# Routed attention with a feed-forward block: the mask products on row tiles of 32 rows in place of 64

## The chip, the cores and the metric

The kernel runs on one core of a Trainium2 chip. The metric is the time of one execution on the device in microseconds. The kernel before was run three times: median 895.17 us, 894.86 to 895.47. One more execution was taken with the hardware profiler; the views below come from it.

## The reference

Queries, keys and values have 4 batches, 8 heads, 768 positions and 64 numbers per head, in float32. Each head has 16 centroids. Every query and every key is assigned to the centroid with the largest cosine, and a query sees only the keys of its own cluster:

```
q_assign = np.argmax(np.einsum('bhsd,hcd->bhsc', q_n, c_n), axis=-1)
k_assign = np.argmax(np.einsum('bhsd,hcd->bhsc', k_n, c_n), axis=-1)
mask = q_assign[:, :, :, None] == k_assign[:, :, None, :]
scores = scale * np.matmul(q, k.transpose(0, 1, 3, 2))
scores = np.where(mask, scores, -1000000000.0)
attn = softmax(scores)            # max taken off, exp, divided by the sum
out = np.matmul(attn, v)
```

The heads are then joined to rows of 512, and a layer norm, a product with 512x2048 weights, a ReLU, a product with 2048x512 weights and an addition of the input follow (the feed-forward part).

## The kernel before

**Heads go in pairs.** There are 16 pairs (4 batches, 4 pairs of heads). The queries of a pair lie transposed in one tile of 128 rows, `t0`, and the keys in another, `t1`: rows 0 to 63 hold the 64 numbers of the first head, rows 64 to 127 those of the second; the 768 positions are the columns. The queries are taken in two halves of 384 columns (`HC`), the keys in 6 blocks of 128. A *step* `(n, g, c)` is pair n, half g, key block c: 16 x 2 x 6 = 192 steps, and the six steps of one half make a *half pair* (a "unit" in the code), 32 in all.

**A step** (`scores`, lines 368 to 389) fills one PSUM tile `s_ps` with two banks, one for each head. It does so with four products on TensorE (line 386):

- two *mask products* in bf16, head j = 0 and j = 1. Their operands are the one-hot cluster tiles `mask[0]` (queries) and `mask[1]` (keys). Each head owns 64 rows of these tiles, from row j * 64 on. Of these, the first 32 (`Q`) hold its one-hots for 16 clusters and those of the other half or head, scaled by 0 or 1; the other 32 rows are set to zero. The key side holds 0 or -2^100, so a pair of positions in different clusters gets a number that the exponential turns into zero.
- two *q·k products* in f32, which are added onto the same banks.

Then ScalarE takes the exponential of both heads at once (line 381, tile `e`). The slice that both kinds of product use is

```
rows = [slice(j * D, (j + 1) * D) for j in range(2)]
```

with D = 64, so head 0 works on rows 0 to 63 and head 1 on rows 64 to 127 of TensorE's array. Such a product occupies a *tile* of the array, 64 rows by 128 columns; products on different rows can run side by side.

**Weighing** (`weigh`, line 398) multiplies the exponentials by v, over 128 rows, into columns 0 to 63 for head 0 and 64 to 127 for head 1 (tiles of 128x64). `finish` (line 452) sums the denominators with tiles of 128x32, and `prep_sims` (line 305) computes the similarities to the centroids, also with tiles of 128x32. `prep_mask` (lines 349 to 355) writes the mask tiles of the next pair. Line 671, `busy`, issues idle products of 128x128 at the start.

**The order is written out by hand** (`manual_schedule`). At the start, three steps are prepared (`AHEAD` = 3): three times q·k alone, then three times the masks with the exponential. Then, for each half pair, come the scores of its six steps (three in the first half pair), one behind the other, each with its mask products ahead of its q·k products; then, in the first half of a pair, the denominators of the pair before and the similarities of the next; then the six weighings. The first mask of a half pair therefore comes behind other products (nearly always weighing), every other mask behind the q·k products of the step before.

**The feed-forward part** follows the attention. Its products (lines 803, 910 and 1093) use the whole array, 128x128.

In the profile PE is TensorE's products, PEld its weight loads. An f32 product shows as two weight loads and two matmul records; a bf16 product shows as one of each.

Of the kernel before, what the change touches and what calls it, by code (L numbers as in the profile page):

```python
# [19 lines left out]
def kernel(  # L20
# [12 lines left out]
    B, H, S, D = q.shape  # L33
# [7 lines left out]
    Q = 32  # L41
# [101 lines left out]
    mask = [heads.tile([P, S], BF16, name=f"mask_{i}", bufs=1) for i in range(2)]  # L143
# [224 lines left out]
    def scores(i, first="mask", parts=("mask", "qk", "exp")):  # L368
        n, g, c = steps[i]
        st = prepared[n]  # L370
        if parts[0] == first:
            st["s", i] = ps_s.tile([P, 2, 512], F32, tag="s", name="s_ps")
        s = st["s", i]
        keys = slice(c * P, (c + 1) * P)
        rows = [slice(j * D, (j + 1) * D) for j in range(2)]
        for part in parts:
            if part == "exp":
                if c % 2 == 0:
                    soft[i // 2] = attn.tile([P, 2, 2, HC], F32, tag="e", name="e", bufs=4)
                e = soft[i // 2][:, c % 2]  # L380
                nc.scalar.activation(e, s[:, :, :HC], AF.Exp, scale=SCALE)  # L381
                continue
            for j in range(2):
                of_queries, of_keys = [(mask if part == "mask" else st)[i][rows[j]] for i in range(2)]
                o = (g ^ j if part == "mask" else g) * HC
                nc.tensor.matmul(  # L386
                    s[:, j, :HC], of_keys[:, keys], of_queries[:, o : o + HC],
                    start=part == first, stop=part != first, skip_group_check=True,
                )
# [119 lines left out]
    rows = {}  # L509
# [155 lines left out]
    with tc.manual_schedule(engines=order | {mybir.EngineType.SP}):  # L665
# [25 lines left out]
        for i in range(AHEAD):  # L691
            scores(i, "qk", ("qk",))
        for i in range(AHEAD):
            scores(i, "qk", ("mask", "exp"))
        load_weight(0)
        load_weight(1)
    with tc.manual_schedule(engines=order | {mybir.EngineType.Pool}):
        for u in range(len(pairs) * slots):
# [9 lines left out]
            for i in own:  # L708
                if i >= AHEAD:
                    scores(i)  # L710
# [609 lines left out]
    with tc.manual_schedule(engines={mybir.EngineType.PE}):  # L1320
        st = {}
# [319 lines left out]
```

## Time and profile before

| what | value |
|---|---|
| median of three runs | 895.17 us |
| the profiled execution, its own time | 896.45 us |
| span of the profiled execution, first to last instruction | 894.6 us |
| mean granted clock of TensorE | 0.998 |
| first and last product of line 386 start at | 9.0 and 324.7 us |
| q·k products (s_ps<-t,t) | 768 records, 154.9 us, mean 483 ns |
| mask products (s_ps<-mask,mask) | 384 records, 63.0 us, mean 324 ns |
| weighing (a_ps<-e,v_sb) | 768 records, 130.9 us, mean 490 ns |
| weight loads of q·k, of the mask | mean 188 ns, mean 94 ns |
| exponentials (line 381, ScalarE) | 192, 151.2 us, mean 813 ns |

A line of a group gives the source line, the engine and the operation, the tiles written and read, the shapes, the count, the busy time in us and the mean length of one record in ns. In the timeline a line is a start, the length of the merged group from its first start to its last end, and a count. Records of products that follow each other overlap, because the array takes in the next product while the last one drains; how fast products follow each other is seen from the differences of their starts. In a table by stretches each engine has its busy time and the count of instructions, in the order PE, PEld, VectorE, ScalarE, GpSimd, followed by the granted clock and the share and rate of the DMA.

### The profile page before, as it was taken

The numbers are of one execution on the slowest core, as the hardware profiler recorded it, in microseconds if no ns is written. First come the engines' busy times: TensorE is split into PE (matmuls) and PEld (weight loads), VectorE is DVE, ScalarE is ACT, GpSimd is POOL, SyncE is SP. The second block draws the span as 40 slices with busy tenths as digits, with TensorE's granted clock in tenths as the row PEclk, the third lists the DMA queues.
The fourth block names the chain that finished last, engine by engine and source line by source line (L and its number), as shares of the span: only waits on it lengthen the run. The fifth ranks groups of instructions, "written<-read, shape, count | busy, mean of one in ns | idle before, by whom it ended". The sixth has DMA issues, their size and how long they took to land.

```text
span 894.6 us, 13278 instructions
## 1 busy us (share of the span) xinstructions
PE 879.7 (98%) x4724; PEld 576.6 (64%) x4724; DVE 701.5 (78%) x1158; ACT 399.7 (45%) x739; POOL 79.3 (9%) x143
## 2 busy tenths in 40 slices
PE   8999999999999999999999999999999999999995
PEld 4444444444444445568886558997557997557995
DVE  6999989899888888889555777897646897645774
ACT  4777777898877753331003552102553111333110
POOL 1122222112111212110000000000000000000000
PEclk9999999999999999999999999999999999999999
DMA  7889999999797536877423558963236862511875
GB/s 154 151 184 176 161 167 193 220 197 180 159 217 129 146 90 181 202 189 244 163 73 134 195 196 302 306 178 91 48 86 183 286 204 54 98 72 36 270 200 99
DMA packets 250489, 147.86 MB, mean 165 GB/s; under 512 B 193568, under 2 KB 209072, under 8 KB 249392
## 3 DMA queue, kind: packets, MB, share of 16 engines
q1 hardware_dynamic: 234784, 130.75, 56.3%
q0 software_dynamic: 7776, 15.03, 8.6%
q10 hardware_dynamic: 7856, 1.16, 0.8%
q8 instruction: 39, 0.64, 0.3%
q14 instruction: 34, 0.28, 0.1%
HBM read 105.25 MB, written 33.25 MB: 155 GB/s over the span
## 4 chain that ended last, share of the span: by engine, by line
PE 64%; DVE 0%; issue 0%
PE x_ps L803 18%; PE x_ps L1093 12%; PE z_ps L803 9%; PE z_ps L1093 6%; PE x_ps L910 5%; PE y_ps L803 5%; PE y_ps L1093 3%; PE z_ps L910 2%; PE y_ps L910 1%; PE s_ps L386 1%; PE a_ps L398 1%; PE den_ps L452 0%; DVE u L1108 0%; DVE y_end L1194 0%; DVE m L1108 0%
## 5 line engine op out<-in xcount | busy, mean ns | idle before, releaser
L381 ACT ACTIVATE e<-s_ps 128x768 f32<-128x768 f32 x192 | 151.2, 813 | 8.8 <-PE s_ps L386 5.0
L386 PE MATMUL s_ps<-t,t 64*128 64x384 f32 x768 | 154.9, 483 | 0.0
L398 PE MATMUL a_ps<-e,v_sb 128*64 128x384 f32 x768 | 130.9, 490 | 0.0
L398 PEld LDWEIGHTS a_ps<-e,v_sb 128*64 128x64 f32 x768 | 52.3, 137 | 75.8 <-issue 62.8
L386 PEld LDWEIGHTS s_ps<-t,t 64*128 64x128 f32 x768 | 68.2, 188 | 34.6 <-issue 33.6
L1093 PE MATMUL x_ps<-lower,w 128*128 128x192 f32 x448 | 80.9, 327 | 1.2 <-DVE u L1108 0.9
L1093 PEld LDWEIGHTS x_ps<-lower,w 128*128 128x128 f32 x448 | 74.0, 190 | 3.1 <-DVE u L1108 1.5
L834 DVE TENSOR_TENSOR lower<-z_ps,u 128x384 f32<-128x384 f32 x56 | 31.0, 553 | 54.7 <-PE z_ps L803 45.9
L386 PE MATMUL s_ps<-mask,mask 64*128 64x384 bf16 x384 | 63.0, 324 | 1.1 <-ACT e L381 0.7
L842 ACT ACTIVATE lower<-lower 128x384 f32<-128x384 f32 x88 | 45.0, 522 | 40.3 <-DVE lower L834 40.3
L433 DVE TENSOR_TENSOR two<-e 128x1536 f32<-128x1536 f32 x30 | 52.6, 1753 | 13.0 <-ACT e L381 12.9
L829 ACT COPY u<-x_ps 128x384 f32<-128x384 f32 x64 | 30.6, 479 | 68.1 <-PE x_ps L803 68.1
L829 ACT COPY p<-x_ps 128x384 f32<-128x384 f32 x32 | 15.1, 471 | 91.1 <-PE x_ps L803 91.1
L436 DVE TENSOR_TENSOR two<-two,e 128x1536 f32<-128x1536 f32 x30 | 52.6, 1752 | 1.7
L386 PEld LDWEIGHTS <-mask 64*128 64x128 bf16 x384 | 19.4, 94 | 42.7 <-issue 11.7
L803 PE MATMUL x_ps<-xn,w 128*128 128x384 f32 x128 | 46.6, 487 | 0.0
L803 PE MATMUL x_ps<-xn,ws 128*128 128x384 f32 x128 | 46.5, 486 | 0.0
L803 PE MATMUL y_ps<-xn,w 128*128 128x384 f32 x128 | 46.5, 486 | 0.0
L803 PE MATMUL x_ps<-xt,ws 128*128 128x384 f32 x128 | 46.5, 486 | 0.0
L803 PE MATMUL z_ps<-xt,ws 128*128 128x384 f32 x128 | 46.5, 486 | 0.0
L803 PE MATMUL x_ps<-xt,w 128*128 128x384 f32 x128 | 46.5, 486 | 0.0
L803 PE MATMUL z_ps<-xn,ws 128*128 128x384 f32 x128 | 46.5, 486 | 0.0
(210 smaller groups left out, 1486.7 us busy)
## 6 DMA issues: line engine op xcount, KB each, us to landing
w<-w_d SPq DMA_DIRECT2D x84, 256.0 KB, 3.7
raw<-in_moe_w_ch_dram SPq DMA_DIRECT2D x32, 512.0 KB, 5.7
w<-w_t SPq DMA_DIRECT2D x36, 256.0 KB, 5.0
w<-tb POOLq DMA_DIRECT2D x32, 256.0 KB, 6.6
w_d<-wt SPq DMA_DIRECT2D x7, 1024.0 KB, 4.7
w<-w_all SPq DMA_DIRECT2D x27, 256.0 KB, 3.0
v_sb<-in_v_dram SPq DMA_DIRECT2D x32, 192.0 KB, 4.7
xr<-x_d SPq DMA_DIRECT2D x24, 256.0 KB, 3.1
```

What stands on the lines that cost most here:

```text
L381: nc.scalar.activation(e, s[:, :, :HC], AF.Exp, scale=SCALE)
L386: nc.tensor.matmul(s[:, j, :HC], of_keys[:, keys], of_queries[:, o : o + HC], start=part == first, stop=part != first, skip_group_check=True,)
L398: nc.tensor.matmul(acc[j * D : (j + 1) * D, :HC], loaded[n]["v"][:, j, c, :], e[:, j, :], start=(c == 0), stop=(c == NT - 1),)
L433: nc.vector.tensor_tensor(two, soft.pop(u), soft.pop(u + 1), ALU.add)
L436: nc.vector.tensor_tensor(two, two, soft.pop(u + 2), ALU.add)
L803: nc.tensor.matmul(bank[:, :HC], lhs[:, c, :], rhs[:, c], start=first and c == 0, stop=c == NDH - 1, skip_group_check=True,)
L829: nc.scalar.copy(t, bank[:, :HC])
L834: nc.vector.tensor_tensor(h, bank[:, :HC], other, ALU.add)
L842: nc.scalar.activation(h, h, AF.Relu)
L910: nc.tensor.matmul(bank[:, :MH].rearrange("p (h f) -> p h f", h=2), hidden[lhs + (c,)][:, tt * P : (tt + 1) * P], rhs[:, :, c], start=firs ...
L1093: nc.tensor.matmul(bank, w[:, c, :], a[:, c], start=way in (1, 2, 5) and c == 0, stop=c == NQH - 1, skip_group_check=True,)
```

## The change

One line of `scores` is replaced by two. The mask products take 32 rows for each head, the one-hots alone: rows 0 to 31 for head 0 and 64 to 95 for head 1. The q·k products keep their 64 rows.

```
             for j in range(2):
-                of_queries, of_keys = [(mask if part == "mask" else st)[i][rows[j]] for i in range(2)]
+                r = slice(j * D, j * D + Q) if part == "mask" else rows[j]
+                of_queries, of_keys = [(mask if part == "mask" else st)[i][r] for i in range(2)]
                 o = (g ^ j if part == "mask" else g) * HC
                 nc.tensor.matmul(
                     s[:, j, :HC], of_keys[:, keys], of_queries[:, o : o + HC],
```

The tile of the array that a product occupies follows from its operands' rows, so the mask products go from tiles of 64x128 (at rows 0 and 64) to tiles of 32x128 (at rows 0 and 64). Line numbers behind the change are one higher in the changed kernel.

More of the change, by code (lines that the diff above doesn't have):

```diff
@@ L383, in scores @@
             for j in range(2):
-                of_queries, of_keys = [(mask if part == "mask" else st)[i][rows[j]] for i in range(2)]
+                r = slice(j * D, j * D + Q) if part == "mask" else rows[j]
+                of_queries, of_keys = [(mask if part == "mask" else st)[i][r] for i in range(2)]
                 o = (g ^ j if part == "mask" else g) * HC
```

## The prediction

> **What bounds the kernel now.** I read the page's busy shares first, then the busy time by stretches, then TensorE's own waits, and last the instructions one by one where TensorE changes from one kind of product to another.
>
> The page, parts 1 and 2:
>
> ```profile
> span 894.6 us, 13278 instructions
> PE 879.7 (98%) x4724; PEld 576.6 (64%) x4724; DVE 701.5 (78%) x1158; ACT 399.7 (45%) x739; POOL 79.3 (9%) x143
> PE   8999999999999999999999999999999999999995
> ```
>
> A busy share alone doesn't prove a bound, since the ends of matmuls are modelled. So I took the attention by itself (18.6 to 310.6 us), and then the list of what PE waited for between 18 and 308 us, which has one line:
>
> ```profile
> 18.60:310.60 292.00, 290.67 (x2069) 133.52 (x2069) 269.54 (x354) 233.22 (x356) 59.56 (x92) 1.00 0.88 175
> PE s_ps L386 <- ACT e L381: 0.2, 1, 0.2
> ```
>
> PE is busy for 290.67 of 292.00 us, at a granted clock of 1.00, and waits for others for 0.2 us. VectorE with 269.54 and ScalarE with 233.22 have room. After the attention the feed-forward part keeps PE as full (554.26 of the 565 us behind 330). So each nanosecond that PE gains or loses in the attention arrives at the end undiminished; no engine stands by to hide it.
>
> The steady rhythm of the scores, from the timeline of PE (start, length of the merged group, count):
>
> ```profile
> 203.98 0.33 PE L386 MATMUL s_ps<-mask,mask 64*128 64x384 bf16 x2
> 204.14 0.81 PE L386 MATMUL s_ps<-t,t 64*128 64x384 f32 x4
> 204.79 0.33 PE L386 MATMUL s_ps<-mask,mask 64*128 64x384 bf16 x2
> ```
>
> Count by starts, not by lengths, because one matmul's record overlaps the next. A step takes 204.79 - 203.98 = 0.81 us: 0.16 for the two mask products, 0.65 for the two q·k products. Each f32 product is two weight loads and two matmul records, so "x4" is two waves of two heads, 0.322 us apart. The two heads of a wave run side by side, on rows 0-63 and 64-127.
>
> **What the change removes: nothing that costs.** The mask products stay 192 pairs with 384 columns each; only the rows go from 64 to 32 (0-31 and 64-95). Rows don't set the pace here: f32 products over 128 rows (x_ps, eight in 2.58 us in the chain of waits) and over 64 rows (two waves in 0.65 us) both take 0.322 us per 384 columns. The mask's weight load has a mean of 94 ns with 64 rows, and 97 to 98 ns for the 128-row load of the idle products; it lies beside the q·k products. Saved: 0. The order of instructions on all engines is unchanged, and no DMA, wait or buffer is touched. The rows left out of the mask hold zeros, so the products are the same.
>
> **What the change adds: changes of the tile.** In the program built from the changed kernel the mask products have tiles of 32x128, the q·k products still 64x128. Before, mask and q·k had one tile shape, and the timeline shows no gap between them. Nearly all other changes of tile in the trace cost time (the exceptions stand under the free case). Three of them:
>
> ```profile
> 8.63 0.44 PE L671 MATMUL idle_ps<-once 128*128 128x128 bf16 x5
> 9.01 0.92 PE L386 MATMUL s_ps<-t,t 64*128 64x384 f32 x4
> ...
> 208.64 1.14 PE L398 MATMUL a_ps<-e,v_sb 128*64 128x384 f32 x6
> 209.71 0.34 PE L386 MATMUL s_ps<-mask,mask 64*128 64x384 bf16 x2
> 209.88 0.81 PE L386 MATMUL s_ps<-t,t 64*128 64x384 f32 x4
> ...
> 215.65 0.51 PE L305 MATMUL sim_ps<-t,cT 128*32 128x384 f32 x4
> 216.11 0.87 PE L398 MATMUL a_ps<-e,v_sb 128*64 128x384 f32 x4
> ```
>
> - *Into q·k* (first pair; rows alone change, 128 to 64). The idle products follow each other at 0.056 us; the last of five starts at 8.63 + 4 x 0.056 = 8.856, so the next was due at 8.912. It starts at 9.005 (rounded to 9.01 in the line): 0.093 late. Then the group takes 0.92 us where the steady one takes 0.81: 0.105 more, because the first weight load (182 to 187 ns in f32) now starts with its product and not ahead of it. Together **0.198 us**.
> - *Into the mask* (second pair, 128x64 to 64x128). The last wave of a_ps starts at 208.64 + 2 x 0.322 = 209.29, so the next was due at 209.61; it starts at 209.71: 0.103 late by the unrounded starts. The q·k products follow 0.172 behind it and not 0.162: 0.010 more, as the bf16 load is short. Together **0.113 us**.
> - *Between two sizes of small tile* (third pair, columns 32 to 64). Due at 215.65 + 0.32 = 215.97, seen at 216.11: 0.14 late; then 0.87 for a group that steadily takes 0.81: 0.05. Together 0.19 us.
>
> The count. Of the 192 steps, three are prepared at the start (q·k first, then the masks): one change into the mask, which falls into a wait for the mask at 11.6 us and costs nothing. The three left of the first half pair have three changes into q·k and two into the mask. Each of the other 31 half pairs has six into q·k and five into the mask; its first mask comes behind other products, a change that is there already. So 3 + 186 = 189 into q·k and 2 + 155 = 157 into the mask, 346 in all.
>
> The sum: 189 x 0.198 = 37.4 us and 157 x 0.113 = 17.7 us, **55.1 us**. The profiled execution took 896.45 us (1.85 around its span) and would take 951.6; the median of the runs shown is 1.28 us lower, so 950.3 us, 6.2% slower. A step would take 0.81 + 0.31 = 1.12 us.
>
> The trace has no change between 64 and 32 rows, so the price is an estimate from the nearest rows. From below, as long as a change costs at all, only the lateness of the next product counts, 0.093 us each time (the smallest of the three): 346 x 0.093 = 32 us, 927 us. From above, each of the 346 costs what the dearest did, 0.198: 68.5 us, 964 us. I take the two prices by kind, because the first pair differs from the change's own case only in the number of rows, and because the added load time follows the load's length in all three (182 to 187 ns: 0.105; 133 ns: 0.05; 92 ns: 0.01). No change at all, and a gain, stand below as rivals. I cost the other engines at nothing: their work in a step (ScalarE's exponential 0.813 us) then has more room than now.
>
> The Trainium skill, page "TensorEngine Tiling (Array Packing)", section Key Properties, states that changing the tiling mode, not just the tile, drains the TensorE, and its list of configurations has 64x128 and 32x128 as two of them. By it the unseen case would pay like the seen ones, and the sum stands. The same page, section Theoretical Speedup, promises up to 4x for a contraction of 32 or less, against 2x up to 64; by it the mask pairs would take 0.08 us and not 0.16, 15 us less in all, about 880 us. That presupposes four products in four row tiles; the code still issues two. No run here shows it yet.
>
> **The rivals.**
>
> *Free change* (6%, 895 us, within 0.2%). The array might let 32-row and 64-row tiles follow each other without waiting, as both are row tiles of 128 columns. For it: two products on different rows start 3 ns apart now, and the few transposes that use fewer columns of the array (ct_ps with 64, stat_ps with 12 among the feed-forward products) keep the full array's pace, so not every difference in shape costs. Against it: those are transposes; every change between plain products costs, also the one from 32 to 64 columns, where both sides are small tiles of one kind: 0.19. It decides if the lateness per change is under 0.005 us (346 x 0.005 = 1.7 us, 0.2%).
>
> *Overlap, faster* (3%, about 865 us). A 32-row product leaves half of its former rows free, and the mask products could run beside the q·k products: 189 x 0.16 = 30 us saved. For it: disjoint rows do run together. Against it: q·k takes rows 0-63 and 64-127, which include 0-31 and 64-95, so no q·k product has disjoint rows. It decides if q·k starts under 0.16 us behind its mask with no lateness.
>
> *The pair falls apart* (7%, about 980 us). The two 32-row products of a pair might run one behind the other: 189 x 0.16 = 30 us on top of the 55. For it: no 32-row pair is in the trace. Against it: four 32-column tiles (sim_ps) start 7 ns apart, and the two heads write different banks.
>
> **How the numbers follow.** Tile changes at prices between 0.093 and 0.198 us have 84%, with 950.3 us as the likeliest; free 6%, faster 3%, falling apart 7%. The range 927 to 964 us holds the first case and leaves 16% out. Faster by over 0.2% (what a measurement of this kernel can tell from no change): 0.03; within: 0.06; slower: 0.91.
>
> **What would show it.** In the profile after, a step of the scores should be 1.12 us from mask to mask: q·k starts 0.25 us behind the mask (0.16 + 0.09), its group is 0.92 long, and the next mask starts 0.09 later than due. The weight loads of both should begin with their products and no longer ahead of them. The attention should end near 384 us and the stretch behind it be as long as now. Wrong if q·k still starts 0.16 behind the mask (free), earlier (overlap), or if the two records of a mask pair start 0.16 us apart (falling apart).

## The result and the profile after

The changed kernel takes 949.78 us (median of four, 948.58 to 952.24) against 895.32 us (four, 894.86 to 895.63): ratio 1.0612, 95% interval 1.0591 to 1.0634. That is 54.5 us; the forecast was 55.1 us, 950.3 in all.

The profiled execution took 952.24 us, span 950.4. The page's first two parts:

```profile
span 950.4 us, 13278 instructions
PE 936.2 (99%) x4724; PEld 568.2 (60%) x4724; DVE 702.2 (74%) x1158; ACT 405.0 (43%) x739; POOL 78.5 (8%) x143
PE   8999999999999999999999999999999999999996
```

The number of instructions is the same on each engine. VectorE is busy as long as before (702.2 us, 701.5 before), ScalarE 5 us longer, PE 56 us longer. PE's list of waits between 18 and 360 us is empty: it waits for no other engine. The groups of instructions show the waits of the others (the idle time stands behind the second bar); the first two lines are of the kernel before, the others of the changed one:

```profile
L381 ACT ACTIVATE e<-s_ps 128x768 f32<-128x768 f32 x192 | 151.2, 813 | 8.8 <-PE s_ps L386 5.0
L433 DVE TENSOR_TENSOR two<-e 128x1536 f32<-128x1536 f32 x30 | 52.6, 1753 | 13.0 <-ACT e L381 12.9
...
L381 ACT ACTIVATE e<-s_ps 128x768 f32<-128x768 f32 x192 | 155.2, 810 | 60.4 <-PE s_ps L387 59.2
L387 PE MATMUL s_ps<-t,t 64*128 64x384 f32 x768 | 176.9, 539 | 0.0
L434 DVE TENSOR_TENSOR two<-e 128x1536 f32<-128x1536 f32 x30 | 52.7, 1758 | 55.5 <-ACT e L381 55.5
L387 PE MATMUL s_ps<-mask,mask 32*128 32x384 bf16 x384 | 64.7, 333 | 1.0 <-ACT e L381 0.6 <-ACT mask L351 0.4
```

ScalarE's exponentials now sit idle for 59.2 us until their scores arrive (5.0 us before), and VectorE's sums for 55.5 us until the exponentials do (12.9 before). That is what a slower bound looks like from the engines behind it.

The timeline of PE in a half pair, where each step shows the price:

```profile
222.45 0.33 PE L387 MATMUL s_ps<-mask,mask 32*128 32x384 bf16 x2
222.72 0.92 PE L387 MATMUL s_ps<-t,t 64*128 64x384 f32 x4
223.57 0.34 PE L387 MATMUL s_ps<-mask,mask 32*128 32x384 bf16 x2
223.83 0.92 PE L387 MATMUL s_ps<-t,t 64*128 64x384 f32 x4
224.68 0.34 PE L387 MATMUL s_ps<-mask,mask 32*128 32x384 bf16 x2
```

From mask to mask there are 1.113 us (median over the trace; 0.808 before). q·k starts 0.26 behind its mask, not 0.16, and its group is 0.92 long, not 0.81. PE's busy digits hide all of this: they read 9 in both kernels, because the modelled records cover the gaps. The starts tell where the time goes; the busy time counts it as work.

The weight loads of the same stretch:

```profile
222.72 0.30 PEld L387 LDWEIGHTS s_ps<-t,t 64*128 64x128 f32 x4 [0.17 <-issue]
223.56 0.10 PEld L387 LDWEIGHTS <-mask 32*128 32x128 bf16 x2 [0.54 <-issue]
223.83 0.30 PEld L387 LDWEIGHTS s_ps<-t,t 64*128 64x128 f32 x4 [0.17 <-issue]
```

They begin with their products (222.72, 223.56, 223.83). In the kernel before they ran ahead:

```profile
203.98 0.35 PEld L386 LDWEIGHTS s_ps<-t,t 64*128 64x128 f32 x4 [0.23 <-issue]
204.47 0.10 PEld L386 LDWEIGHTS <-mask 64*128 64x128 bf16 x2
204.79 0.35 PEld L386 LDWEIGHTS s_ps<-t,t 64*128 64x128 f32 x4 [0.23 <-issue]
```

There the q·k loads begin at 203.98 us for products at 204.14, and the mask's loads at 204.47 for products at 204.79. The loads have not become longer (the mask's 91 ns, 94 before), they have only lost their cover.

The feed-forward part begins at 385.89 us (329.91 before) and lasts 564.5 us from there (564.7 before). The whole difference lies in the attention. In this one execution the granted clock was 0.86 in the first 24 us, and 1.00 in the same stretch before. That fits its span having grown by 55.8 us where the medians differ by 54.5.

### The profile page after: what moved, and what is told of

The parts are those of the page before. It is cut to its first block, busy times and chain, and to the rows that moved or that the text cites. A ratio compares the mean times of both kernels' runs of the same rounds, so it can differ in the third digit from the quotient of the medians.

```text
span 950.4 us, 13278 instructions
## 1 busy us (share of the span) xinstructions
PE 936.2 (99%) x4724; PEld 568.2 (60%) x4724; DVE 702.2 (74%) x1158; ACT 405.0 (43%) x739; POOL 78.5 (8%) x143
## 4 chain that ended last, share of the span: by engine, by line
PE 61%; DVE 0%; issue 0%
PE x_ps L804 17%; PE x_ps L1094 12%; PE z_ps L804 9%; PE z_ps L1094 6%; PE x_ps L911 4%; PE y_ps L804 4%; PE y_ps L1094 3%; PE z_ps L911 2%; PE s_ps L387 1%; PE y_ps L911 1%; PE a_ps L399 1%; PE den_ps L453 0%; DVE u L1109 0%; DVE y_end L1195 0%; DVE m L1109 0%
## 5 line engine op out<-in xcount | busy, mean ns | idle before, releaser
L381 ACT ACTIVATE e<-s_ps 128x768 f32<-128x768 f32 x192 | 155.2, 810 | 60.4 <-PE s_ps L387 59.2
L387 PE MATMUL s_ps<-t,t 64*128 64x384 f32 x768 | 176.9, 539 | 0.0
L434 DVE TENSOR_TENSOR two<-e 128x1536 f32<-128x1536 f32 x30 | 52.7, 1758 | 55.5 <-ACT e L381 55.5
L387 PEld LDWEIGHTS <-mask 32*128 32x128 bf16 x384 | 18.2, 91 | 107.0 <-issue 89.9
L387 PEld LDWEIGHTS s_ps<-t,t 64*128 64x128 f32 x768 | 58.4, 186 | 33.7 <-issue 33.0
L387 PE MATMUL s_ps<-mask,mask 32*128 32x384 bf16 x384 | 64.7, 333 | 1.0 <-ACT e L381 0.6
```

The lines of the kernel that those rows point to most:

```text
L387: nc.tensor.matmul(s[:, j, :HC], of_keys[:, keys], of_queries[:, o : o + HC], start=part == first, stop=part != first, skip_group_check=True,)
L434: nc.vector.tensor_tensor(two, soft.pop(u), soft.pop(u + 1), ALU.add)
```

## The experiments

The theory (A): what costs is the change of the tile's shape between 32 and 64 rows. Each time the next product is late by some 0.09 to 0.10 us, and its first weight load is exposed. The rival (B): a product on 32 rows, or its weight load, is slow by itself, 55 us over 192 pairs. The changed kernel alone can't tell these apart, since each of its 32-row pairs has a change on either side. Later rivals: the shape matters only on the rows that a product uses (A2); the price is flat and does not depend on the length of the load (D).

### Fewer changes, as many 32-row products: the alternating order

Each second step takes q·k first and the mask behind it:

```
             for i in own:
                 if i >= AHEAD:
-                    scores(i)
+                    if i % 2:
+                        scores(i, "qk", ("qk", "mask", "exp"))
+                    else:
+                        scores(i)
```

With 32 rows:

> Mask products on 32 rows as in the changed kernel, but every second step takes its q·k products first and its mask behind them, so that masks of neighbouring steps stand side by side: 95 changes of the tile into q·k and 95 into the mask, in place of 189 and 157. The number of 32-row products and of columns is the same. Theory A (each change of the tile between 64 and 32 rows costs: 0.207 us into q·k and 0.100 into the mask, as read from the changed kernel's trace): 95 x 0.307 = 29 us over the kernel before, 924 us. Rival B (a 32-row product or its weight load is slow by itself, about 55 us / 192 = 0.28 us for each pair): 950 us, as the changed kernel.

The same order with 64 rows:

> The same order of steps as the alternating one, with mask products on 64 rows: no change of the tile between mask and q·k. Theory A: 895 us as the kernel before, within 2 us. If the order by itself costs or gains something (waits on the score buffers or on the exponentials), it shows here, and then the alternating 32-row kernel is to be compared with this one. Rival B: 895 us as well.

Measured: 923.3 us with 32 rows (ratio to the kernel before 1.0322, 1.0305 to 1.0339), and 894.95 us with 64 rows (1.0006, 0.9996 to 1.0016, no difference). The order costs nothing, and 190 changes in place of 346 cost 28.4 us in place of 54.5: 0.298 us for each of the 95 pairs of changes. B wanted 950 and is out. The timeline of the alternating 32-row kernel:

```profile
216.53 0.33 PE L387 MATMUL s_ps<-mask,mask 32*128 32x384 bf16 x2
216.79 1.56 PE L387 MATMUL s_ps<-t,t 64*128 64x384 f32 x8
218.28 0.50 PE L387 MATMUL s_ps<-mask,mask 32*128 32x384 bf16 x4
218.71 1.56 PE L387 MATMUL s_ps<-t,t 64*128 64x384 f32 x8
220.21 0.50 PE L387 MATMUL s_ps<-mask,mask 32*128 32x384 bf16 x4
```

Two mask pairs side by side take 0.50 us. They start 0.173 us apart, where two pairs of 64 rows start 0.162 apart; the 0.01 more is the exposed load of the first pair, and between 32-row pairs nothing else is lost. The 1.56 of eight q·k records are 0.92 for the first four and 0.64 for the others: the price falls on the first after a change, and on no other.

### One change each way per half pair: the bunched order

The masks of three steps, then q·k of all six, then the other three masks:

```
-            for i in own:
-                if i >= AHEAD:
-                    scores(i)
+            todo = [i for i in own if i >= AHEAD]
+            early3, late3 = (todo[:3], todo[3:]) if len(todo) == NT else (todo, [])
+            for i in early3:
+                scores(i, "mask", ("mask",))
+            for i in early3:
+                scores(i, "mask", ("qk", "exp"))
+            for i in late3:
+                scores(i, "qk", ("qk",))
+            for i in late3:
+                scores(i, "qk", ("mask", "exp"))
```

With 32 rows:

> Mask products on 32 rows; in each half pair the masks of three steps, then the q·k products of all six, then the masks of the other three: one change into q·k and one into the mask per half pair, 32 and 31 in all. Theory A: 32 x 0.207 + 31 x 0.100 = 9.7 us over the same order with 64 rows; with no waits from the bunched exponentials that is 905 us. Rival B: 55 us over the same order with 64 rows, 950 us.

With 64 rows:

> The bunched order with mask products on 64 rows, no change of the tile. Theory A and rival B: 895 us if the order brings no waits; each exponential of the second three steps comes up to three steps later, which may cost some us by the score buffers (three of them) or by VectorE's sums. The difference of the bunched 32-row kernel to this one is what tells A from B.

Measured: 926.8 us with 32 rows (1.036, 1.0343 to 1.0378) and 917.9 us with 64 rows (1.0249, 1.0232 to 1.0266). The difference that tells A from B is 8.9 us, where A said 9.7 and B 55. That it comes so near to 9.7 is partly luck. In the two traces nearly all second halves of pairs take 0.30 us longer over their scores with 32 rows (A: 0.307), but most first halves, in which both kernels wait, only 0.11. Another 2.0 us come from one half pair, in which the granted clock of the 32-row kernel was 0.51 (337 to 344 us). The hope for an order without waits was wrong: the order costs 23 us by itself, more than the changes that it saves against the alternating one. The timeline of the bunched 64-row kernel, parts of two half pairs, shows where:

```profile
200.79 4.46 PE L386 MATMUL s_ps<-t,t 64*128 64x384 f32 x24
...
206.33 0.83 PE L305 MATMUL sim_ps<-t,cT 128*32 128x384 f32 x8
208.08 4.09 PE L398 MATMUL a_ps<-e,v_sb 128*64 128x384 f32 x24 [0.93 <-ACT dsb L461]
...
212.60 4.04 PE L386 MATMUL s_ps<-t,t 64*128 64x384 f32 x24
```

Three exponentials queue up on ScalarE behind the last masks, and the copy of the denominators (dsb, line 461) stands behind them. Weighing, which needs the bank that this copy frees, starts at 208.08 and not at 207.11 (0.78 behind the start of sim_ps, as in the other kernels). The q·k groups of the first half pair stretch from 4.04 to 4.46 us, as the score buffers (three `s_ps` tiles) come free later. The starts in the traces of this kernel and of the kernel before split most of the cost. The second halves of pairs take as long as before, but for one. Of the 16 first halves 15 take 0.69 to 0.89 us longer over their scores, as their masks and q·k products stretch: about 13 us in all, the one second half included. Weighing comes 0.32 us later in ten of them and 0.97 in four, 7 us in all. Together that is 20 of the 22.4 us by which the feed-forward part starts later (352.26 and 329.91 us). No run takes these waits away one by one.

### One head on 32 rows, the other on 64

```
-                r = slice(j * D, j * D + Q) if part == "mask" else rows[j]
+                r = slice(j * D, j * D + Q) if part == "mask" and j else rows[j]
```

> Only head 1's mask product takes 32 rows (64 to 95); head 0's keeps 64 (0 to 63). Theory A1 (the shape of the tile is one setting of the whole array, so a change waits for all products in flight): head 1's mask can no longer run beside head 0's: 0.162 us more, then a change between them (0.092 + 0.010) and one into q·k (0.092 + 0.105), 0.461 us in each of 189 steps, 87 us: 982 us, dearer than the full change. Theory A2 (the shape matters only on the rows that a product uses): head 0's stream has no change and head 1's pays at most what it pays in the changed kernel: 950 us or less. Rival B (32-row products slow by themselves): between 895 and 950 us.

Measured: 981.3 us (1.0963, 1.0944 to 1.0981). A1 said 982; A2 and B said 950 or less. Half of the change costs more than all of it. The timeline:

```profile
220.69 0.59 PE L387 MATMUL s_ps<-mask,mask 64*128 64x384 bf16 x2
221.20 0.92 PE L387 MATMUL s_ps<-t,t 64*128 64x384 f32 x4
221.95 0.59 PE L387 MATMUL s_ps<-mask,mask 64*128 64x384 bf16 x2
```

(The group is named by its first record; the second has 32 rows.) The pair takes 0.59 us in place of 0.33: head 1's mask starts 0.255 us behind head 0's, which is 0.162 for the 384 columns and 0.093 for the change. Two products on different rows, which elsewhere start 3 ns apart, no longer run side by side once their row counts differ. From head 0's mask back to q·k on the same 64 rows nothing would have to change, and still it comes 0.26 us behind head 1's mask: here the shape acts as one setting for the whole array.

### The mask in f32: a longer load behind the change

```
-    mask = [heads.tile([P, S], BF16, name=f"mask_{i}", bufs=1) for i in range(2)]
+    mask = [heads.tile([P, S], F32, name=f"mask_{i}", bufs=1) for i in range(2)]
```

With 64 rows:

> The kernel before with the mask tiles in f32: each mask product becomes two waves of 0.322 us in place of one of 0.162, 0.48 us more in each of 192 steps, 93 us: 988 us. No change of the tile, so no load is exposed between mask and q·k. It is the base for the next kernel; at the start of a half pair the longer load (187 ns and not 94) costs about 0.1 us x 31 = 3 us more, 991 us.

With 32 rows:

> The f32 mask on 32 rows. Theory A with an exposed weight load (a change makes the first load start with its product, so the price follows the load's length): a change into the mask now costs what one into q·k does, 0.2 us: 189 x 0.2 + 157 x 0.2 = 69 us over the f32 mask with 64 rows. Rival D (the price is a flat wait that doesn't depend on the load that follows; q·k is dearer for another reason): 55 us over it, as in bf16. Rival B: 55 us or more, by the longer products up to four times as much.

Measured: 990.5 us with 64 rows (1.1069, 1.105 to 1.1087) and 1063.0 with 32 (1.1871, 1.1843 to 1.1898). The difference is 72.5 us; A with exposed loads said 69, the flat price 55. The timelines of PE, first with 64 rows, then with 32:

```profile
244.14 0.81 PE L386 MATMUL s_ps<-mask,mask 64*128 64x384 f32 x4
244.78 0.81 PE L386 MATMUL s_ps<-t,t 64*128 64x384 f32 x4
245.43 0.81 PE L386 MATMUL s_ps<-mask,mask 64*128 64x384 f32 x4
```

```profile
243.29 0.91 PE L387 MATMUL s_ps<-mask,mask 32*128 32x384 f32 x4
244.13 0.92 PE L387 MATMUL s_ps<-t,t 64*128 64x384 f32 x4
244.98 0.91 PE L387 MATMUL s_ps<-mask,mask 32*128 32x384 f32 x4
```

Mask groups now stretch from 0.81 to 0.91 as q·k groups do, and a step from 1.290 to 1.690 us: 0.20 for each of its two changes. In bf16 the change into the mask stretched nothing that could be seen (0.33 and 0.34). So the second half of the price is the load: the f32 mask's first load takes 181 ns and adds 0.105, the bf16 mask's takes 91 and adds 0.010. That it goes by the length and not by the type alone is seen in weighing, whose f32 load of 64 columns takes 133 ns and adds 0.05 (0.87 for the first four records from 205.69 us on in the kernel before, not 0.81). Of the 72.5 us, 346 x 0.2 gives 69. The rest falls at the start: in the traces the scores of each later half pair take 2.20 us longer, 11 changes at 0.20, but the first half pair takes 5.8 us longer, where its five changes come to 1.0. The granted clock of the 32-row execution was 0.50 from 14.4 to 24.5 us, where the 64-row one had 1.00. The one execution with 32 rows whose mean clock was as high as the base's (0.997) took 1059.1 us, 68.6 more than the base.

## Why the prediction was right

- **The bound.** "Each nanosecond that PE gains or loses in the attention arrives at the end undiminished" held: 54.5 us more at the end, no wait of PE to take any of it back, and a feed-forward part of the same length (564.5 and 564.7 us).
- **Nothing saved.** In the bunched order the second and third of three neighbouring mask pairs start 0.163 us apart with 32 rows, and 0.163 with 64. The load went from 94 to 91 ns, and those 3 ns were hidden before and are too few to count now.
- **Into q·k**, forecast 0.093 late and 0.105 for the load. Measured 0.092 (0.264 between the starts of 222.453 and 222.717, of which 0.162 are columns and 0.010 the mask's own load) and 0.105 (0.427 between the two q·k waves, not 0.322).
- **Into the mask**, forecast 0.103 and 0.010; measured 0.100 (0.422 between the last q·k wave and the mask, not 0.322) and 0.010. The row taken for it came from a change out of 128x64 tiles; it was 3 ns off.
- **The third row, outside the sum,** was read too high. Weighing starts 0.05 us behind the end of the copy dsb in 14 half pairs of the kernel before, so its 0.14 holds a wait for ScalarE. The one place without this copy (17.48 us) is 0.11 late. Together with the load that is 0.16 us and not 0.19. The argument that the row served, that a change between two small tiles costs too, stands.
- **The count.** 189 changes into q·k and 158 into the mask stand in the trace (one of these in the wait at the start). With the measured prices 189 x 0.197 + 157 x 0.110 = 54.5 us; the medians differ by 54.5.
- **The rivals.** The free change, the overlap and the pair that falls apart did not occur in the changed kernel: q·k is later, not on time or earlier, and the two masks of a pair start 3 ns apart. The mixed kernel shows that the last of them was a real danger, with another cause: a pair falls apart when its two tiles differ in shape. The reason against the free change (that 32 and 64 columns, both small tiles, cost too) carried over from columns to rows.
- **The rule that spoke against the change.** The Trainium skill, page "TensorEngine Tiling (Array Packing)", section Key Properties, has it that a change of the tiling mode, not merely of the tile, drains the TensorE. The runs agree that such a change costs, and give the price: 0.092 to 0.100 us, plus what the first load can no longer hide. That the array drains meanwhile they don't show, as the ends of the records are modelled. The same page's speedup for a contraction of 32 or less (Theoretical Speedup, up to 4x) is shown by no run here, as none has four row tiles at work.

What was not known before the change, and was assumed, was that a step from 64 to 32 rows pays like one from 128 to 64. It does.

## What to carry to other kernels

Count the changes of the tile's shape along the order of the products, not only the products. Here each cost about 0.1 us and the cover of the next weight load (0.2 us together in front of an f32 product with 128 columns). A step's two changes cost 0.31 us, and its mask products only 0.16: even a tile that made them free would have lost. Keep one shape over neighbouring products, padding with zero rows if need be, or bring those of one shape together (padding was the faster here); and give products that are to run side by side the same shape. See first that the order that brings them together doesn't make products wait for another engine: the bunched order by itself cost 23 us.

## What the runs showed that I had not expected

- Putting only one head on 32 rows costs 86 us, more than putting both there (54 us).
- The lateness hardly depends on the type of the product that ends: 0.092 us behind bf16 masks, 0.100 behind f32 q·k. The difference between the prices comes from the load of the product that begins (0.010 and 0.105).
- The alternating order (with 64 rows, 894.95 us) is as fast as the order before; no kernel here was faster than the one before. Putting q·k on 32 rows as well, so that no change is left, was not tried.
